# H3 long convolution and SwiGLU on one core: block 0's second norm from PSUM, paired down rows, new instruction orders

## Chip, cores and metric

The kernel runs on one core of one Trainium2 chip. The metric is the device time of one execution in microseconds. Three executions of the kernel before took 274.61 us in the median (273.61 to 275.37).

## What is computed

Two sublayers on a sequence of 2048 tokens with 640 channels, all in bfloat16. `_layernorm` subtracts the mean and divides by the square root of variance plus 1e-5.

```python
def _A_ref(q, k, v, shift_k, ssm_k, ssm_D):
    ...
    for t in range(ks):                                  # ks = 4
        k_shift = k_shift + k_pad[:, t:t + S, :] * shift_k[:, ks - 1 - t][None, None, :]
    kv = k_shift * v
    ...                                                  # y: causal convolution of kv with ssm_k over 2048 tokens, by FFT
    y = y + kv * ssm_D[None, None, :]
    return q * y

def _B_ref(x, w_gate, w_up, w_down):                     # 640 -> 1728 -> 640
    g = _silu(x @ w_gate)
    u = x @ w_up
    return (g * u) @ w_down

x = A_q
h = x + _A_ref(_layernorm(x, axis=-1), A_k, A_v, A_shift_k, A_ssm_k, A_ssm_D)
h2 = h + _B_ref(_layernorm(h, axis=-1), B_w_gate, B_w_up, B_w_down)
```

## The kernel before

The 2048 tokens are cut into four blocks of 512. The long convolution becomes a block convolution: every block of kv (`xf0` to `xf3`) and every block of the filter (`kf0` to `kf3`) is taken through a half-sample-shifted Fourier transform of 512 points by matrix products, spectra are multiplied on VectorE (`prod(j, i)`, for j up to i), and the inverse transform (`iv0` to `iv3`) gives the block's output. The feed-forward layer then runs on the block (`ffn`).

For a block the stages are:

- `kv` (L548, L543, L554): the four-tap filter of k as products with diagonal matrices, on TensorE in 64x64 tiles for the first four channel groups and in one full tile for the fifth, evicted by ScalarE; five transposing DMAs (`kvt`) bring it back to token rows in `kvo`; VectorE multiplies it into `vt` (L563).
- `halves` (L502, L514): eight transforms of four 320-column matmuls, for two frequency halves f, even or odd samples and cosine or sine. ScalarE evicts each; VectorE adds and subtracts even and odd (`bfly`, L491). For `kf0` alone the kernel before is "direct": the odd results aren't evicted, VectorE adds them from PSUM (L510).
- `prod`: products with the filter's spectra (L576, L577), their sums (L579, L581), added to `Y` (L584); behind the last one, `bfly` makes the inputs `IE` and `IO` of the inverse.
- `inverse` (L637): four tiles of 128 tokens. For each, ScalarE copies PSUM with the bias 1/std of the first norm into `qo` (L648), VectorE multiplies with the normalised x (L650) which gives h, ScalarE takes the row sum (L652) and the sum of squared deviations (L654), GpSimd adds epsilon and takes the power -1/2 (L656, L658), VectorE normalises (L660), and a transposing DMA (`hn`) writes `hnT`.
- `ffn`: fourteen groups of hidden rows, thirteen of 128 and one of 64. A group of 128 is ten 512-column matmuls (L681, L682); the last holds 64 gate and 64 up columns in five (L692). ScalarE applies silu (L699) and copies the up part (L701), VectorE multiplies them (L703). The last group's product goes to rows 64 to 127 of `gz`, whose other rows are zero. Then, for four tiles of 128 tokens, 14 row groups times two column halves of 320 are accumulated (L715), VectorE adds the result to h (L721) and SP stores it.

All accumulators come from one pool of four PSUM tiles of two banks each (`units=4`). A tile is taken when the first matmul into it is issued and given back when its last reader is done. ScalarE does most evictions.

Every engine's instruction order is written out. `g.add` gives every operation a number as the program is traced; the `ORDER` lists name these numbers per engine (TensorE, ScalarE, VectorE, GpSimd, and SP for DMA issues), and an engine takes its list strictly in that order, waiting on semaphores. `schedule` only walks through the lists to assign the PSUM tiles. The cost in each `g.add` belongs to the search that made the lists, which isn't part of the program.

In the lists before, TensorE takes all of kv0, kf0 but one transform and four kf1 transforms ahead of xf0; the remaining filter transforms and kv1 stand around iv0; the feed-forward of a block overlaps with the next block's VectorE products.

Of the kernel before, what the change touches and what calls it, by code (L numbers as in the profile page):

```python
# [10 lines left out]
ALU = mybir.AluOpType  # L11
ACTF = mybir.ActivationFunctionType
P = 128
# [15 lines left out]
class _Tile:  # L29
# [8 lines left out]
    def f(self, b, n, parts=slice(0, P)):  # L38
        o = self.unit * 1024 + b * 512
        return self.g.ps[parts, o:o + n]  # L40

# [13 lines left out]
class _Graph:  # L55
# [148 lines left out]
    def emit(self, block):  # L204
# [74 lines left out]
    """,  # L279
    "act": """  # L280
# [10 lines left out]
    """,  # L291
    "dve": """
# [10 lines left out]
    """,  # L303
    "pool": """
        8 5 6 7 147 148 149 150 151 204 205 196 220 197 221 212 213 327 328 329 408 409 400 384 401 392 385 393 506 507 508 581
        597 582 598 589 573 590 574 695 696 697 780 796 781 797 772 773 788 789
    """,
    "sp": """
# [7 lines left out]
def bass_sequential_preLN__ssm_conv_h3__swiglu_ffn__prompt_kernel(  # L316
# [31 lines left out]
    ftab_d = nc.inline_tensor(_to_bf16(np.stack([np.cos(angx), np.sin(angx)], 1).reshape(P, -1)), name="cst_ftab")  # L348
    itab_d = nc.inline_tensor(_to_bf16(np.stack([np.cos(angi), np.sin(angi)], 1).reshape(P, -1)), name="cst_itab")
# [4 lines left out]
    with ExitStack() as es:  # L354
# [56 lines left out]
        KO = [sb("KO%d" % m, p, [2, 2, D]) for m, p in enumerate((w + 10240, S[4], w + 10240, S[4] + 5120))]  # L411
        o = w + 17920
# [4 lines left out]
        mv = [sb("mv%d" % i, o + 320 + 32 * i, [4], f32) for i in range(4)]  # L417
# [3 lines left out]
        BN, DIRECT = (0,), ('kf0',)  # L421
# [26 lines left out]
        load("ftab", ftab[:], ftab_d.ap().rearrange("p (a j c) -> p a j c", a=2, j=4), 524288)  # L448
        load("itab", itab[:], itab_d.ap().rearrange("p (a f j c) -> p a f j c", a=2, f=2, j=4), 524288)
# [5 lines left out]
        g.add("pool", "gz", lambda e: e.memset(gz[0:H, :], 0.0), 500, w=[gz[0:H, :]])  # L455
# [36 lines left out]

        def halves(cls, name, src, ev, od, scale, direct=False):
# [23 lines left out]
        def kfwd(m, dst):  # L517
            halves("kf", "kf%d" % m, KT[m], dst, KO[m], D ** 0.5 / N, "kf%d" % m in DIRECT)
            for f in range(0 if "kf%d" % m in DIRECT else 2):
                bfly("kf%d" % m, dst[:, f], KO[m][:, f], dst[:, f], dst[:, f + 2], 2 * D)  # L520

        def kcomb(dst, own, prev, m):
            g.add("dve", "kc%d" % m, lambda e: e.tensor_tensor(out=dst[:, :, 0, :], in0=own[:, :, 0, :], in1=prev[:, :, 1, :], op=ALU.add),
                  cdve(4 * D), r=[own[:, :, 0, :], prev[:, :, 1, :]], w=[dst[:, :, 0, :]])
            g.add("dve", "kc%d" % m, lambda e: e.tensor_tensor(out=dst[:, :, 1, :], in0=own[:, :, 1, :], in1=prev[:, :, 0, :], op=ALU.subtract),
                  cdve(4 * D), r=[own[:, :, 1, :], prev[:, :, 0, :]], w=[dst[:, :, 1, :]])

        def kv(i):
# [6 lines left out]
            for a in range(3):  # L535
# [17 lines left out]
                ks = kT[:, c0:c0 + nb, 0:N]  # L553
                g.add("act", nm, lambda e, pt=pt, ks=ks, nb=nb: e.activation(  # L554
# [244 lines left out]
```

## Time and profile before

| | |
|---|---|
| median of 3 runs | 274.61 us |
| the profiled execution | 276.58 us |
| its span, first to last instruction | 274.6 us |
| TensorE busy | 255.8 us (93%) |
| VectorE busy | 210.5 us (77%) |
| ScalarE busy | 187.9 us (68%) |
| GpSimd busy | 37.8 us (14%) |
| mean granted TensorE clock | 0.981 |

The profile shows one execution. An instruction's line (L715) is its line in the kernel printed above. Busy time counts when an engine executes; matmuls are pipelined, so that successive ones overlap in the records and the step from start to start is what one costs. An arrow in brackets gives the idle time in front of an instruction and what ended it.

### The profile page before, as it was taken

Reading aid. Unit: us, or ns where it says so; the run is one execution under the profiler, and the core shown is the slowest. Engines: PE = TensorE matmul, PEld = TensorE weight load, DVE = VectorE, ACT = ScalarE, POOL = GpSimd, SP = SyncE. Lnnn points to the kernel's source line nnn. Section 1 sums busy time; section 2 is a strip of 40 time slices with the busy share of each in tenths; the row PEclk is TensorE's granted clock in tenths of the full one; section 3 lists DMA queues with packets and bytes.
Section 4 is the critical chain, followed back from the end, with each engine's and each line's share of the span. In section 5 each row is a group of like instructions: output and inputs, shape, how many; then the busy total and the mean of one; then the engine's idle time right before and its main releaser. Section 6 shows DMA issues by size and latency. Waiting matters only on the chain.

```text
span 274.6 us, 4036 instructions
## 1 busy us (share of the span) xinstructions
PE 255.8 (93%) x1596; PEld 143.4 (52%) x1596; DVE 210.5 (77%) x281; ACT 187.9 (68%) x338; POOL 37.8 (14%) x54
## 2 busy tenths in 40 slices
PE   0998767899899999999999999999999999999995
PEld 0566434354544566754444666644446774444673
DVE  1479997987999999999999999999999413212222
ACT  1798998989966799167978892667769911546400
POOL 1002302900040011100040054000500220000000
PEclk9999989599999999999999999999999999999999
DMA  7999974274900073463100415530000050200002
GB/s 171 318 175 319 381 272 98 48 118 102 376 17 0 0 169 85 94 170 114 46 1 2 98 21 124 143 98 0 0 0 2 1 121 2 72 0 2 0 24 72
DMA packets 45204, 26.49 MB, mean 96 GB/s; under 512 B 34945, under 2 KB 43906, under 8 KB 45186
## 3 DMA queue, kind: packets, MB, share of 16 engines
q1 hardware_dynamic: 44528, 26.23, 35.2%
q8 instruction: 12, 0.20, 0.3%
q10 hardware_dynamic: 658, 0.01, 0.1%
q14 instruction: 6, 0.05, 0.1%
HBM read 15.69 MB, written 2.62 MB: 67 GB/s over the span
## 4 chain that ended last, share of the span: by engine, by line
PE 58%; DVE 25%; ACT 9%; DMA 6%; SPq 1%; issue 1%; DVEq 0%
PE ps L681 16%; PE ps L682 16%; PE ps L715 11%; PE ps L502 6%; DVE tt L577 4%; DMA kvo<-kT 4%; DVE tt L576 4%; PE ps L637 3%; PE ps L548 2%; DVE X L491 2%; DMA ident<-cst_id 2%; DVE xh L721 2%; DVE vt L563 2%; PE ps L692 2%; ACT qo L648 2%; DVE Y L584 2%
## 5 line engine op out<-in xcount | busy, mean ns | idle before, releaser
L715 PE MATMUL ps<-Wd,gu 128*128 128x320 bf16 x416 | 59.6, 299 | 0.0
L681 PE MATMUL ps<-hnT,GA 128*128 128x512 bf16 x140 | 53.1, 379 | 0.2 <-ACT ub L701 0.2
L682 PE MATMUL ps<-hnT,UA 128*128 128x512 bf16 x140 | 53.1, 379 | 0.0
L701 ACT ACTIVATE ub<-ps 128x512 bf16<-128x512 f32 (+1 forms) x56 | 32.8, 596 | 25.5 <-PE ps L682 19.3
L715 PEld LDWEIGHTS ps<-Wd,gu 128*128 128x128 bf16 x416 | 40.5, 98 | 17.0 <-DVE gu L703 0.5
L681 PE MATMUL ps<-hnT,GB 128*128 128x512 bf16 x120 | 45.5, 379 | 0.0
L682 PE MATMUL ps<-hnT,UB 128*128 128x512 bf16 x120 | 45.5, 379 | 0.0
L699 ACT ACTIVATE gu<-ps 128x512 bf16<-128x512 f32 x52 | 30.1, 596 | 13.4 <-PE ps L682 13.2
L703 DVE TENSOR_TENSOR gu<-gu,ub 128x512 bf16<-128x512 bf16 x52 | 21.2, 420 | 23.3 <-ACT gu L699 14.0
L576 DVE TENSOR_TENSOR tt<-X,C 128x2560 bf16<-128x2560 bf16 x20 | 29.7, 1484 | 0.1
L577 DVE TENSOR_TENSOR tt<-X,C 128x2560 bf16<-128x2560 bf16 x20 | 29.7, 1484 | 0.1
L502 PE MATMUL ps<-KT,ftab 128*128 128x320 bf16 x128 | 21.7, 316 | 4.0 <-ACT KT L482 1.6
L721 DVE SCALAR_TENSOR_TENSOR xh<-ps,st,xh 128x640 bf16<-128x640 f32 x16 | 14.0, 879 | 14.4 <-PE ps L715 14.4
L681 PEld LDWEIGHTS ps<-hnT,GA 128*128 128x128 bf16 x140 | 13.7, 98 | 17.3 <-ACT ub L701 0.7
L682 PEld LDWEIGHTS ps<-hnT,UA 128*128 128x128 bf16 x140 | 13.7, 98 | 15.7
L514 ACT ACTIVATE FO<-ps 128x640 bf16<-128x640 f32 x16 | 10.7, 705 | 14.3 <-PE ps L502 14.3
L502 PE MATMUL ps<-vt,ftab 128*128 128x320 bf16 x128 | 18.8, 299 | 1.5 <-DVE vt L563 1.4
L682 PEld LDWEIGHTS ps<-hnT,UB 128*128 128x128 bf16 x120 | 11.8, 98 | 14.2
L681 PEld LDWEIGHTS ps<-hnT,GB 128*128 128x128 bf16 x120 | 11.8, 98 | 14.1
L502 PEld LDWEIGHTS ps<-KT,ftab 128*128 128x128 bf16 x128 | 11.5, 101 | 13.2 <-ACT KT L482 2.7
L656 POOL TENSOR_SCALAR mv<-mv 128x1 f32<-128x1 f32 x16 | 6.6, 418 | 85.5 <-ACT qo L654 85.5
L584 DVE TENSOR_TENSOR Y<-Y,tt 128x2560 bf16<-128x2560 bf16 x12 | 17.8, 1486 | 0.1
(73 smaller groups left out, 377.8 us busy)
## 6 DMA issues: line engine op xcount, KB each, us to landing
kc<-in_A_ssm_k_dram SPq DMA_DIRECT2D x4, 640.0 KB, 5.6
xh<-in_A_q_dram SPq DMA_DIRECT2D x4, 640.0 KB, 5.2
vt<-in_A_v_dram SPq DMA_DIRECT2D x4, 640.0 KB, 6.2
out_dram<-xh SPq DMA_DIRECT2D x16, 160.0 KB, 2.0
Wd<-in_B_w_down_dram SPq DMA_DIRECT2D x1, 1280.0 KB, 6.9
UA<-in_B_w_up_dram SPq DMA_DIRECT2D x1, 1120.0 KB, 10.3
GA<-in_B_w_gate_dram SPq DMA_DIRECT2D x1, 1120.0 KB, 14.6
UB<-in_B_w_up_dram SPq DMA_DIRECT2D x1, 960.0 KB, 10.7
```

The source lines that it names most:

```text
L502: last = e.matmul(pt.f(c, W), ftab[:, cs, j, f * P:(f + 1) * P], src[:, j, c * W:(c + 1) * W], start=(j == par), stop=(j == par + 2))
L514: g.add("act", name, lambda e, pt=pt, d=d: e.activation(out=d.rearrange("p (b x) -> p b x", b=2), in_=pt.f2(W), func=ACTF.Copy, scale=scal ...
L576: g.add("dve", nm, lambda e, x=x, k=k: e.tensor_tensor(out=t1, in0=x, in1=k, op=ALU.mult), cdve(2560), r=[x, k], w=[t1])
L577: g.add("dve", nm, lambda e, x=x, k=ksw: e.tensor_tensor(out=t2, in0=x, in1=k, op=ALU.mult), cdve(2560), r=[x, k], w=[t2])
L584: g.add("dve", nm, lambda e, yy=yy: e.tensor_tensor(out=yy, in0=yy, in1=tacc, op=ALU.add), cdve(2560), r=[yy, tacc], w=[yy])
L681: e.matmul(pt.f(0, N), wg[:, c, f0:f0 + P], hnT[:, c, :], start=(c == 0), stop=(c == NC5 - 1))
L682: last = e.matmul(pt.f(1, N), wu[:, c, f0:f0 + P], hnT[:, c, :], start=(c == 0), stop=(c == NC5 - 1))
L699: g.add("act", nm, lambda e, pt=pt, gv=gv, a=ps_g: e.activation(out=gv, in_=pt.f(a[0], N, a[1]), func=ACTF.Silu, scale=D ** 0.5), cact(N), ...
L701: g.add("act", nm, lambda e, pt=pt, uv=uv, a=ps_u: e.activation(out=uv, in_=pt.f(a[0], N, a[1]), func=ACTF.Copy, scale=D ** 0.5), cact(N), ...
L703: g.add("dve", nm, lambda e, uv=uv, gv=gv: e.tensor_tensor(out=gv, in0=gv, in1=uv, op=ALU.mult), cdve(N), r=[gv, uv], w=[gv])
L715: last = e.matmul(pt.f(c, W), slots[fb][:, j * P:(j + 1) * P], Wd[:, fb, c * W:(c + 1) * W], start=(fb == 0), stop=(fb == 13))
L721: g.add("dve", nm, lambda e, pt=pt, x2=x2, m=m: e.scalar_tensor_tensor(out=x2, in0=pt.f2(W), scalar=m, in1=x2, op0=ALU.subtract, op1=ALU.add),
```

## The change

Operations that are numbered anew, and three edits that change what is executed (the branches for `R4`, `D8`, `PT` and `BN2`, whose switches are empty, add nothing):

- `ST = (0,)`: in block 0's second norm one VectorE `scalar_tensor_tensor` reads the inverse's tile from PSUM, adds the bias, multiplies with x, writes h and its row sum. ScalarE's copy, VectorE's product and ScalarE's row sum go. GpSimd takes the mean from the sum with one more operation a tile; the squares are taken of the row sum minus 640 h, so that epsilon and the scale in front of silu (`gain`) change by powers of 640.
- `PAIR = True`: the last hidden group's product is made in two halves: tokens 0 to 255 in rows 64 to 127 of `gz`, tokens 256 to 511 in rows 0 to 63. The last 64 rows of `Wd` are loaded twice, one half each. In the down product, 13 row groups are accumulated with full tiles; the last 64 rows of token tiles j and j + 2 are done together, one in the upper 64 array rows and one in the lower. The clearing of `gz` goes.
- `DIRECT = ()`: kf0 goes the way of the other transforms: all eight results are evicted by ScalarE and VectorE adds and subtracts in SBUF.
- `ORDER`: all five lists are new.

```diff
-        BN, DIRECT = (0,), ('kf0',)
+        BN, DIRECT, D8, PT, BN2, ST, R4, PAIR = (0,), (), (), (), (), (0,), (), True
...
+                if st:
+                    x2 = x.rearrange("p (b x) -> p b x", b=2)
+                    g.add("dve", nm, lambda e, pt=pt, x2=x2, s=s, j=j, m=m: e.scalar_tensor_tensor(
+                        out=x2, in0=pt.f2(W), scalar=s[:, 3, j:j + 1], in1=x2, op0=ALU.add, op1=ALU.mult, accum_out=m[:, 4:5]),
+                          cps(D) + 120, r=[x, s[:, 3, j:j + 1]], w=[x, m[:, 4:5]], pr=[pt])
+                    g.add("pool", nm, lambda e, m=m: e.tensor_scalar(out=m[:, 0:1], in0=m[:, 4:5], scalar1=-1.0 / D, scalar2=None, op0=ALU.mult),
+                          400, r=[m[:, 4:5]], w=[m[:, 0:1]])
+                    g.add("act", nm, lambda e, x=x, m=m, q=q: e.activation(out=q[:], in_=x, func=ACTF.Square, scale=-float(D), bias=m[:, 4:5],
+                                                                          accum_out=m[:, 1:2]), cact(D, 1) + 115,
+                          r=[x, m[:, 4:5]], w=[q[:], m[:, 1:2]])
...
+                parts = [(rows, ps_g, ps_u, slice(0, N))]
+                if fb == 13 and PAIR:
+                    parts = [(slice(H, P), ps_g, ps_u, slice(0, N // 2)), (slice(0, H), ps_g, ps_u, slice(N // 2, N))]
...
+            for j in ((0, 2, 1, 3) if PAIR else range(4)):
...
+                if PAIR and not second:
+                    dn[j + 2] = g.tile("dn")
+
+                    def mm(e, j=j, ta=dn[j], tb=dn[j + 2]):
+                        for c in range(2):
+                            for t, row, k in ((ta, H, j), (tb, 0, j + 2)):
+                                last = e.matmul(t.f(c, W), gz[row:row + H, k * P:(k + 1) * P], Wd[row:row + H, 13, c * W:(c + 1) * W],
+                                                start=(row == 0), stop=(row == H), tile_position=(row, 0))
+                        return last
...
+        if PAIR:
+            for h in range(2):
+                load("Wd", Wd[H * h:H * h + H, 13, :], B_w_down[F - H:F, :], 81920)
```

The new lists, in the names used above, around the first block:

- TensorE: kv0's third part stands behind six kf0 transforms; one kf1 transform stands ahead of xf0 and four stand inside it; xf0's four f = 0 transforms come first. iv0's first three tiles, three filter transforms, the fourth tile, then ten filter transforms mixed with kv1, and three gu0 groups ahead of xf1 instead of four.
- VectorE: iv0's four PSUM operations with three kf1 additions between the third and the fourth; block 1's product with kv (L563) ahead of the first L703, and five kf additions and product steps behind it.
- SP: one half of the last `Wd` rows ahead of ftab; GB loaded early and GA behind kT1.
- In every block the two pairs stand next to each other, behind the full-tile matmuls of the first two token tiles and ahead of those of the other two.

More of the change, by code (lines that the diff above doesn't have):

```diff
@@ L40, in f, with flat @@
         return self.g.ps[parts, o:o + n]
+    def flat(self, n, at=0):
+        o = self.unit * 1024 + at
+        return self.g.ps[:, o:o + n]
     def f2(self, n):
@@ L491, in bfly, with eighths, mm @@
                 g.add("dve", name, lambda e, d=d, op=op: e.tensor_tensor(out=d, in0=e_, in1=o_, op=op), cdve(n), r=[e_, o_], w=[d])
+        def eighths(cls, name, src, dst, scale):
+            for f in range(4):
+                for cs in range(2):
+                    pt = g.tile(cls)
+                    def mm(e, pt=pt, f=f, cs=cs):
+                        fs = slice((f % 2) * P, (f % 2 + 1) * P)
+                        for j in range(4):
+                            for c in range(2):
+                                tab = ntab[:, cs, j // 2, fs] if f > 1 and j % 2 else ftab[:, cs, j, fs]
+                                last = e.matmul(pt.f(c, W), tab, src[:, j, c * W:(c + 1) * W], start=(j == 0), stop=(j == 3))
+                        return last
+                    g.add("pe", name, mm, cpe(W, 8), r=[ftab[:, cs], src] + ([ntab[:, cs]] if f > 1 else []), pw=[pt])
+                    d = dst[:, f, cs, :]
+                    g.add("act", name, lambda e, pt=pt, d=d: e.activation(out=d.rearrange("p (b x) -> p b x", b=2), in_=pt.f2(W),
+                                                                         func=ACTF.Copy, scale=scale), cact(D), w=[d], pr=[pt])
         def halves(cls, name, src, ev, od, scale, direct=False):
@@ L520, in kfwd, with quarters, mm @@
                 bfly("kf%d" % m, dst[:, f], KO[m][:, f], dst[:, f], dst[:, f + 2], 2 * D)
+        def quarters(cls, name, src, ev, od, scale):
+            for r in range(4):
+                for cs in range(2):
+                    pt = g.tile(cls)
+                    def mm(e, pt=pt, r=r, cs=cs):
+                        for c in range(2):
+                            last = e.matmul(pt.f(c, W), ftab[:, cs, r, 0:P], src[:, r, c * W:(c + 1) * W], start=True, stop=True)
+                        return last
+                    g.add("pe", name, mm, cpe(W, 2), r=[ftab[:, cs], src[:, r, :]], pw=[pt])
+                    d = od[:, r // 2, cs, :] if r % 2 else ev[:, r, cs, :]
+                    g.add("act", name, lambda e, pt=pt, d=d: e.activation(out=d.rearrange("p (b x) -> p b x", b=2), in_=pt.f2(W),
+                                                                         func=ACTF.Copy, scale=scale), cact(D), w=[d], pr=[pt])
@@ new lines, in tt2, with pick, spread @@
+        def tt2(name, op, out, a_, b_):
+            g.add("dve", name, lambda e: e.tensor_tensor(out=out, in0=a_, in1=b_, op=op), cdve(2 * D), r=[a_, b_], w=[out])
+        def pick(t, off, step):
+            return bass.AP(t[:].tensor, t[:].offset + off * D, [list(t[:].ap[0]), [step * D, 2], [1, D]])
+        def spread(name, x, o_):
+            tt2(name, ALU.add, x[:, 1], o_[:, 0], o_[:, 1])
+            tt2(name, ALU.subtract, o_[:, 0], o_[:, 0], o_[:, 1])
+            tt2(name, ALU.add, x[:, 3], x[:, 0], x[:, 2])
+            tt2(name, ALU.subtract, o_[:, 1], x[:, 0], x[:, 2])
+            tt2(name, ALU.add, x[:, 0], x[:, 3], x[:, 1])
+            tt2(name, ALU.subtract, x[:, 2], x[:, 3], x[:, 1])
+            tt2(name, ALU.subtract, pick(x, 2, 5), o_[:, 1], pick(o_, 1, -1))
+            tt2(name, ALU.add, pick(x, 6, -3), o_[:, 1], pick(o_, 1, -1))
@@ L553, in kv, with tr @@
                 ks = kT[:, c0:c0 + nb, 0:N]
+                if i in PT:
+                    g.add("act", nm, lambda e, pt=pt, ks=ks, nb=nb: e.activation(out=ks, in_=pt.f2(N)[:, 0:nb], func=ACTF.Copy),
+                          cact(N * nb), w=[ks], pr=[pt])
+                    tp = g.tile("kt")
+                    def tr(e, tp=tp, c0=c0, nb=nb):
+                        for j in range(4):
+                            for b in range(nb):
+                                src = kT[:, c0 + b, j:j + 509:4]
+                                last = e.matmul(tp.flat(P, P * (nb * j + b)), src, ident[:, 0:P] if b == 0 else iswap, start=True, stop=True)
+                        return last
+                    g.add("pe", nm, tr, 70 * 4 * nb, r=[ks, ident[:, 0:P]], pw=[tp])
+                    d = vt[:, :, P * c0:P * (c0 + nb)]
+                    g.add("dve", nm, lambda e, tp=tp, d=d, nb=nb: e.tensor_tensor(
+                        out=d, in0=tp.flat(4 * P * nb).rearrange("p (j x) -> p j x", j=4), in1=d, op=ALU.mult), cps(4 * P * nb),
+                          r=[d], w=[d], pr=[tp])
+                    continue
                 g.add("act", nm, lambda e, pt=pt, ks=ks, nb=nb: e.activation(
@@ L668, in ffn @@
             nm = "ff%d" % i
+            gain = D ** 1.5 if i in ST else D ** 0.5
             slots = []
@@ L715, in mm @@
                                 last = e.matmul(pt.f(c, W), slots[fb][:, j * P:(j + 1) * P], Wd[:, fb, c * W:(c + 1) * W],
-                                                start=(fb == 0), stop=(fb == 13))
+                                                start=(fb == 0 and not second), stop=(fb == 13 or second and fb == 12))
                         return last
```

133 lines of the change are left out of this document (95 added, 38 removed), and 58 rows, old and new, of the table ORDER.

## The prediction

> **What bounds the kernel now.** I read the busy time by stage first, then the TensorE timeline where that table shows holes. Columns: window, length, busy us (and instructions) of TensorE, its weight loads, VectorE, ScalarE and GpSimd, granted clock, DMA share, GB/s.
>
> ```profile
> 21.40:39.40 18.00, 13.84 (x116) 8.90 (x116) 17.71 (x24) 17.10 (x26) 4.39 (x5) 0.99 1.02 359
> 39.40:60.00 20.60, 17.52 (x109) 9.08 (x110) 18.51 (x24) 17.96 (x36) 8.19 (x8) 0.76 0.39 81
> 60.00:70.00 10.00, 9.30 (x45) 4.20 (x45) 7.77 (x13) 9.97 (x20) 0.00 (x0) 1.00 0.67 140
> 70.00:210.00 140.00, 139.66 (x841) 76.54 (x839) 138.20 (x172) 103.13 (x195) 20.99 (x25) 1.00 0.28 73
> 210.00:271.40 61.40, 61.40 (x371) 35.83 (x368) 17.73 (x35) 26.25 (x51) 3.24 (x8) 1.00 0.11 30
> ```
>
> TensorE has no hole after 70 us: whatever is won must come from its work, or from the first 70 us. But VectorE is as full: 138.2 of 140 us between 70 and 210, so TensorE cannot be pulled forward alone. The timeline shows them meet, TensorE starting right behind VectorE, at the input of block 1's forward transform (L563, then L502) and of the last inverse (L491, then L637):
>
> ```profile
> 68.12 1.28 DVE L563 TENSOR_TENSOR vt<-vt,kvo 128x512 bf16<-128x512 bf16 x2
> ...
> 69.47 4.52 PE L502 MATMUL ps<-vt,ftab 128*128 128x320 bf16 x32 [0.70 <-DVE vt L563]
> 73.82 0.38 PE L681 MATMUL ps<-hnT,GA 128*128 128x512 bf16 x1
> ...
> 208.12 1.55 DVE L491 TENSOR_TENSOR IO<-Y 128x1280 bf16<-128x1280 bf16 x2
> ...
> 209.72 2.52 PE L637 MATMUL ps<-IO,itab 128*128 128x320 bf16 x16
> ```
>
> So the end moves by what VectorE gains up to 209.7, plus what TensorE saves after it. From 69.47 to 73.82 I also take the price of one 320-column matmul: 4.35/32 = 0.136 us, 0.54 for a four-matmul transform.
>
> **The change, part by part.**
>
> *Block 0's transform.* Read off the new lists, the four f = 0 transforms of xf0 come first; before, their results left PSUM second, fourth, fifth and sixth.
>
> ```profile
> 11.48 7.60 SPq L442 DMA_TRANSPOSE kvo<-kT  x5
> ...
> 21.37 2.35 PE L502 MATMUL ps<-vt,ftab 128*128 128x320 bf16 x16 [0.72 <-DVE vt L563]
> 22.13 2.49 ACT L514 ACTIVATE X<-ps 128x640 bf16<-128x640 f32 x4 [0.68 <-PE ps L502]
> 26.17 2.42 DVE L491 TENSOR_TENSOR X<-X,FO 128x1280 bf16<-128x1280 bf16 x3 [0.19 <-ACT FO L514]
> ```
>
> Four evictions end at 22.13 + 2.49 = 24.6, so the VectorE chain of block 0 can start at 24.6 instead of 26.17: **1.5 us**. Its 14.6 us of products are the same. Against this, kv0's third part now stands behind six kf0 transforms on TensorE and five kf0 evictions on ScalarE, and its transpose is the last of the five on SP. Those five take 7.6 us to issue, so the fifth cannot start before about 17; kv0's first two parts are evicted by 13 (before SP's second issue), and five evictions of 0.62 and its own put the third at about 16.8. I take no loss; up to 1 us is possible. Of the two Wd half loads (80 KB each instead of one of 160) one stands ahead of ftab on SP, in front of loads and before the transposes: one more issue, covered by SP's wait for kv0's first eviction.
>
> *kf0 without direct evictions:* eight VectorE operations from PSUM (0.82 us each) become four additions (2.42/3 = 0.81) and four ScalarE evictions (0.62). All of it lies ahead of 24.6, where VectorE has room (9.7 of 15.2 us busy before 21.4); ScalarE pays 2.5 us. No gain taken.
>
> *Second norm of block 0.* Price rows, 39.4 to 60 us, and the two forms of the PSUM operation:
>
> ```profile
> L648 ACT ACTIVATE qo<-ps,st 128x640 bf16<-128x640 f32 x4 | 3.2, 788 | 1.3 <-PE ps L637 1.3
> L652 ACT ACTIVATE qo<-xh 128x640 bf16<-128x640 bf16 x4 | 2.9, 729 | 0.0
> L652 ACT ACTIVATION_READ_ACCUMULATOR qo<-xh 128x1 f32 x4 | 0.8, 191 | 0.0
> L650 DVE TENSOR_TENSOR xh<-xh,qo 128x640 bf16<-128x640 bf16 x4 | 2.0, 498 | 1.6 <-ACT qo L648 1.6
> L577 DVE TENSOR_TENSOR tt<-X,C 128x2560 bf16<-128x2560 bf16 x2 | 3.0, 1481 | 0.0
> L656 POOL TENSOR_SCALAR mv<-mv 128x1 f32<-128x1 f32 x4 | 2.8, 699 | 16.8 <-ACT qo L654 16.8
> L510 DVE SCALAR_TENSOR_TENSOR C<-ps,C 128x640 bf16<-128x640 f32 x8 | 6.5, 817 | 0.7 <-ACT C L514 0.7
> L721 DVE SCALAR_TENSOR_TENSOR xh<-ps,st,xh 128x640 bf16<-128x640 f32 x16 | 14.0, 879 | 14.4 <-PE ps L715 14.4
> ```
>
> ScalarE loses L648 and L652: 6.9 us, less the 2.5 above. VectorE gives up four L650 (2.0 us) for four operations whose sum output no row shows: at least L510's 0.82, at most L721's 0.88 plus an accumulator read of 0.19 as ScalarE's, 1.07. So 1.3 to 2.3 us more; I take **2.2**, since L721 has the same pointer scalar and the sum must be read out. In return VectorE no longer waits for ScalarE here. Its longest waits between 40.8 and 69.4 us, and that stretch as a whole:
>
> ```profile
> 42.58 0.49 DVE L650 TENSOR_TENSOR xh<-xh,qo 128x640 bf16<-128x640 bf16 x1 [1.03 <-ACT qo L648]
> ...
> 55.26 0.45 DVE L660 TENSOR_SCALAR qo<-xh,mv 128x640 bf16<-128x640 bf16 x1 [0.46 <-POOL mv L658]
> ...
> 65.24 0.43 DVE L703 TENSOR_TENSOR gu<-gu,ub 128x512 bf16<-128x512 bf16 x1 [1.61 <-ACT ub L701]
> ```
>
> ```profile
> 40.80:69.40 28.60, 24.89 (x144) 12.05 (x142) 24.28 (x34) 25.93 (x51) 8.19 (x8) 0.85 0.49 98
> ```
>
> The stretch holds 28.6 - 24.3 = 4.3 us of idle. The waits for L648 go with it; the longest goes because the new list puts block 1's kvmul (L563) ahead of the first gmul (L703); I leave 1.0 for new ones: **3.3** back. GpSimd gets four more small operations for the mean (0.7 us each at this stage's L656 mean); they run beside ScalarE's squares, and the normalisations (L660) that need them have products and k additions between them.
>
> Sum at kvmul1: 1.5 + 3.3 - 2.2 = **2.6 us**. Can TensorE follow? iv0 starts at 37.9; four iv, thirteen k transforms and kv1 are 14.5 us, to 52.4. On VectorE the first PSUM operation starts at 40.1 (iv0's first tile 1.1 us, one addition), four of them and three additions end at 46.5, four normalisations (0.4) with three operations of L577's size between end at 52.5; the transpose lands 2.6 later (hnT row): gu0 at 55 instead of 59.96. Three gu0 groups of ten 0.216 matmuls end at 61.5; kvmul1, since the new list puts 4.7 us of additions and products behind it, at 69.4 - 2.6 - 4.7 = 62.1. TensorE waits about 0.6 us: VectorE decides. GA's load is moved behind kT1's transposes, at about 44; the DMA engines are 39% busy there, so its 1120 KB land before 55, if the issue row's 14.6 us, taken at full queues, does not repeat (44 + 14.6 = 58.6: still before 59.96).
>
> *Pairs.* The two transfers just named, then TensorE around kv2, where 64x64 tiles are used, and its last down group:
>
> ```profile
> hnT<-qo SPq DMA_TRANSPOSE x16, 2.6
> GA<-in_B_w_gate_dram SPq DMA_DIRECT2D x1, 1120.0 KB, 14.6
> ...
> 101.39 0.98 PE L715 MATMUL ps<-Wd,gu 128*128 128x320 bf16 x6
> 102.21 0.43 PE L715 MATMUL ps<-Wd,gz 128*128 128x320 bf16 x2
> 102.57 1.92 PE L548 MATMUL ps<-kT,dg 64*64 64x512 bf16 x32
> 104.43 1.04 PE L543 MATMUL ps<-kT,dl 128*128 128x512 bf16 x4
> 105.30 0.30 PE L715 MATMUL ps<-Wd,gu 128*128 128x320 bf16 x1
> ...
> 267.44 3.69 PE L715 MATMUL ps<-Wd,gu 128*128 128x320 bf16 x26
> 270.97 0.43 PE L715 MATMUL ps<-Wd,gz 128*128 128x320 bf16 x2
> ```
>
> A full 512-column matmul takes (105.30 - 104.43)/4 = 0.217 us. The 32 small ones of that length start within 1.86 us; one by one they would take 6.9, so four run at once, and I take two 64x128 ones to run at once. The step into the mode costs 102.57 - 102.21 - 2 x 0.136 = 0.09, the step out about as much: eight steps of 0.217 make 1.74 of the 1.86. A round trip is about 0.21. A block loses eight 0.136 matmuls (1.09) and gains four slots (0.54) and, since the new list has both pairs next to each other, one round trip: **0.33 us less**. If halves do not overlap: 0.21 more. The pairs hold four PSUM tiles at once, all there are; the seven matmul groups ahead of them are time enough for kv's evictions. The split of the last gmul into two halves costs VectorE 0 to 0.3 a block, I take 0.08.
>
> [...]
>
> *Sum.* 2.6 at kvmul1; 0.8 of the 1.8 us that VectorE idles from 70 to 210; less 0.24 for three split gmuls: 3.2 at 209.7. Behind it blocks 2 and 3 save 0.33 each: **3.9 us**. The profiled execution took 276.58 us with a span of 274.6 (2.0 around it), so 272.7 on its own scale; it lay 2.0 above the median of the runs shown, 274.61, and on that scale the forecast is **270.7**, 269.2 (the 2.2 at 1.3, and 0.6 more of the waits back) to 271.9 (0.2 more lost, and the input 1.0 late).
>
> **The rivals.**
>
> *A cold TensorE at the start.* The granted clock falls to half behind thin stretches:
>
> ```profile
> 17.00:20.70 3.70, 3.29 (x23) 1.68 (x20) 2.75 (x6) 3.49 (x6) 0.00 (x0) 1.00 0.71 76
> 36.00:39.40 3.40, 1.31 (x8) 0.62 (x8) 3.40 (x6) 3.40 (x7) 0.00 (x0) 0.94 0.93 354
> 39.40:43.00 3.60, 3.60 (x16) 2.17 (x17) 2.57 (x5) 2.52 (x5) 0.00 (x0) 0.58 0.03 10
> 46.00:49.40 3.40, 1.04 (x4) 0.31 (x4) 3.37 (x3) 3.40 (x11) 2.98 (x3) 0.98 0.48 109
> 49.40:55.40 6.00, 5.36 (x32) 2.10 (x36) 5.50 (x9) 5.99 (x11) 5.21 (x6) 0.50 0.34 64
> ```
>
> 39% and 31% busy were thin enough. The new list takes three kf1 transforms (1.6 us) from the stretch before xf0: 1.66 busy from 17 to 21.4, 38%. At half clock the four transforms take 2.2 more and eat the 1.5: 272.2. [...]
>
> *TensorE decides, not VectorE:* if VectorE's waits after 60 us vanish too, the 5.0 us at gu0 and four blocks of 0.33 count: 268.3. Against: VectorE's 138 of 140.
>
> *Pairs that do not run side by side:* blocks 2 and 3 cost 0.42 instead of saving 0.66: 271.8. Against: the 32 matmuls above.
>
> *Slower: TensorE, ahead of VectorE, idles in lumps.* Its list is fixed, so where it waits for VectorE at xf1, xf2, xf3 and iv3 for over about 1.6 us in a stretch, the clock halves for 3.4 us and costs 1.7, as at 39.4. The first lump eats slack; with all four, 6.8 us go, against the 3.9 of the forecast: 277.5. For: two such lumps stand in the trace now. Against: gu groups of 2.2 us fill the lists around these points.
>
> **How the numbers follow.** Forecast 0.45, cold start 0.22, TensorE decides 0.10, pairs 0.07, lumps 0.16. A measurement of this kernel tells about 1% from no change. Below 271.9 lie nearly all of the first, third and fourth and a third of the cold start: 0.61; above 277.4 more than half of the lumps: 0.11; within 1%: 0.28. The range 267.8 to 275.2 leaves out the lumps and the lowest tail.
>
> **What would show it.** Right: the first block 0 addition (L491, X) near 24.6; the four PSUM operations at 0.9 to 1.1 us; gu0's first matmul near 55; iv3 near 206.5; pair matmuls two at a time, 0.136 a step; 6.9 us less of L648 and L652. Wrong: xf0 at a clock under 1.0, a VectorE idle over 2 us between 40 and 62, holes in TensorE after 70, or gu0 not before 58.

## The result, and the profile after

The changed kernel took **292.46 us** (median of four runs, 292.31 to 295.01) against 274.99 (273.61 to 275.74) for the kernel before on the same chip: a ratio of **1.067, 95% interval 1.060 to 1.073**. It is slower, where 270.7 was forecast. (Ratios here leave disturbed executions out on both sides, so they are not always the quotient of the two medians.) The profiled execution took 295.01 us with a span of 293.0.

The busy time by stage first, in the columns of the prediction's first table (length, TensorE, weight loads, VectorE, ScalarE, GpSimd, granted clock, DMA share, GB/s):

```profile
27.70:60.00 32.30, 26.82 (x219) 16.06 (x218) 30.50 (x40) 29.42 (x46) 10.03 (x14) 1.00 0.76 213
60.00:82.20 22.20, 20.95 (x110) 10.29 (x109) 21.12 (x29) 19.26 (x38) 0.00 (x0) 1.00 0.46 144
82.20:95.00 12.80, 9.38 (x44) 4.05 (x42) 12.70 (x14) 4.26 (x8) 12.78 (x1) 1.00 0.00 0
95.00:103.00 8.00, 4.39 (x17) 2.52 (x18) 0.85 (x2) 4.24 (x7) 1.87 (x2) 0.57 0.00 0
103.00:209.70 106.70, 104.33 (x653) 56.90 (x652) 101.90 (x130) 75.48 (x151) 19.49 (x20) 1.00 0.31 69
209.70:220.60 10.90, 10.82 (x57) 5.28 (x55) 10.79 (x13) 4.29 (x9) 10.89 (x1) 1.00 0.00 0
220.60:232.50 11.90, 6.32 (x28) 3.59 (x29) 3.83 (x8) 8.72 (x15) 1.87 (x2) 0.71 0.01 2
```

Before, TensorE had no hole after 70 us. Now there are two, at 90 to 103 and 220 to 232, and the clock halves in both (0.57 and 0.71 as the mean of the stretches, 0.50 for 6.8 us in each). What is striking is the GpSimd column: in the stretch ahead of each hole it is busy from end to end with one single instruction. The groups of the page name it, and ScalarE's wait for it:

```profile
L719 POOL TENSOR_SCALAR st<-st 128x4 f32<-128x4 f32 x4 | 26.6, 6647 | 84.3 <-ACT jk L716 84.2
L728 ACT ACTIVATE xh<-xh,st 128x640 bf16<-128x640 bf16 x16 | 14.6, 933 | 14.3 <-POOL st L724 14.3
```

L719 adds epsilon to 128x4 numbers, the row sums of squares of a block's first norm. The same instruction before (timeline of GpSimd and VectorE, kernel before; L613 is that line there):

```profile
77.60 1.49 DVE L576 TENSOR_TENSOR tt<-X,C 128x2560 bf16<-128x2560 bf16 x1
79.00 0.82 DVE L581 TENSOR_TENSOR tt<-tt 128x1280 bf16<-128x1280 bf16 x1
...
78.54 0.64 POOL L613 TENSOR_SCALAR st<-st 128x4 f32<-128x4 f32 x1 [23.31 <-ACT jk L610]
```

And in block 1 of the changed kernel, timelines of GpSimd, VectorE, ScalarE and TensorE one after the other:

```profile
82.21 12.78 POOL L719 TENSOR_SCALAR st<-st 128x4 f32<-128x4 f32 x1 [26.70 <-ACT jk L716]
95.07 1.67 POOL L722 TENSOR_TENSOR st<-st,half 128x8 f32<-128x8 f32 x1
...
82.12 1.48 DVE L680 TENSOR_TENSOR tt<-X,C 128x2560 bf16<-128x2560 bf16 x1
83.52 0.81 DVE L500 TENSOR_TENSOR IO<-Y 128x1280 bf16<-128x1280 bf16 x1
...
93.42 1.48 DVE L602 TENSOR_TENSOR C<-C,R 128x2560 bf16<-128x2560 bf16 x1
98.50 0.42 DVE L840 TENSOR_TENSOR gu<-gu,ub 128x512 bf16<-128x512 bf16 x1 [3.60 <-ACT ub L838]
...
97.06 0.92 ACT L728 ACTIVATE xh<-xh,st 128x640 bf16<-128x640 bf16 x1 [7.72 <-POOL st L724]
97.89 0.58 ACT L838 ACTIVATE ub<-ps 128x512 bf16<-128x512 f32 x1
...
98.61 4.36 PE L745 MATMUL ps<-IO,itab 128*128 128x320 bf16 x16 [7.03 <-ACT ub L838]
```

Before, GpSimd's add ended 0.09 us after the VectorE operation during which it was asked for. Now it ends 0.10 us after the thirteenth operation behind that one (94.99 against 94.90): it got in only when VectorE had nothing left to do. ScalarE's list has the normalisation L728 ahead of the copies L838, so ScalarE stands still for 7.72 us, no PSUM tile is freed, TensorE waits 7.03 us, and the sixteen matmuls behind it run at half clock (4.36 us for 2.2). VectorE went dry because its next product (L840) waits for ScalarE's copy L838. So GpSimd waits for VectorE, ScalarE for GpSimd and VectorE for ScalarE, and the circle opened only when VectorE had run out of other work. Block 3 repeats it (10.89 us from 209.70).

### The profile page after: what moved, and what is told of

It is laid out like the page before. It is cut to its first block, busy times and chain, and to the rows that moved or that the text cites. A ratio compares the mean times of both kernels' runs of the same rounds, so it can differ in the third digit from the quotient of the medians.

```text
span 293.0 us, 4053 instructions
## 1 busy us (share of the span) xinstructions
PE 258.5 (88%) x1596; PEld 142.3 (49%) x1596; DVE 209.0 (71%) x285; ACT 184.3 (63%) x338; POOL 62.8 (21%) x57
## 4 chain that ended last, share of the span: by engine, by line
PE 47%; ACT 17%; DVE 13%; POOL 12%; DMA 8%; issue 1%; SPq 1%
PE ps L813 12%; PE ps L814 11%; PE ps L857 10%; POOL st L719 8%; PE ps L529 6%; PE ps L745 4%; ACT ub L838 3%; DMA kvo<-kT 2%; ACT xh L728 2%; POOL mv L789 2%; DMA hnT<-qo 2%; DMA xh<-in_A_q_dram 2%; DMA ident<-cst_id 2%; ACT gu L836 1%; ACT qo L768 1%; ACT qo L781 1%
## 5 line engine op out<-in xcount | busy, mean ns | idle before, releaser
L857 PE MATMUL ps<-Wd,gu 128*128 128x320 bf16 x416 | 58.4, 299 | 0.0
L838 ACT ACTIVATE ub<-ps 128x512 bf16<-128x512 f32 (+1 forms) x60 | 33.5, 567 | 25.6 <-PE ps L814 20.8
L719 POOL TENSOR_SCALAR st<-st 128x4 f32<-128x4 f32 x4 | 26.6, 6647 | 84.3 <-ACT jk L716 84.2
L840 DVE TENSOR_TENSOR gu<-gu,ub 128x512 bf16<-128x512 bf16 x52 | 21.0, 419 | 31.7 <-ACT ub L838 19.7
L529 PE MATMUL ps<-vt,ftab 128*128 128x320 bf16 x128 | 21.8, 326 | 3.3 <-DVE vt L660 3.3
L745 PE MATMUL ps<-IO,itab 128*128 128x320 bf16 x64 | 12.6, 362 | 13.6 <-ACT ub L838 12.6
L728 ACT ACTIVATE xh<-xh,st 128x640 bf16<-128x640 bf16 x16 | 14.6, 933 | 14.3 <-POOL st L724 14.3
L529 PE MATMUL ps<-KT,ftab 128*128 128x320 bf16 x128 | 20.4, 301 | 2.3 <-ACT KT L491 1.2
L785 POOL TENSOR_SCALAR mv<-mv 128x1 f32<-128x1 f32 x16 | 11.4, 710 | 49.3 <-ACT qo L783 49.0
```

The lines of the kernel that those rows point to most:

```text
L529: last = e.matmul(pt.f(c, W), ftab[:, cs, j, f * P:(f + 1) * P], src[:, j, c * W:(c + 1) * W], start=(j == par), stop=(j == par + 2))
L719: g.add("pool", nm, lambda e: e.tensor_scalar(out=s[:, 2, :], in0=s[:, 1, :], scalar1=LN_EPS * D, scalar2=None, op0=ALU.add), 3000 if i el ...
L728: g.add("act", nm, lambda e, j=j, xj=xj: e.activation(out=xj, in_=xj, func=ACTF.Identity, scale=s[:, 4, j:j + 1], bias=s[:, 5, j:j + 1]), ...
L745: last = e.matmul(pt.f(c, W), itab[:, cs, f, j, :], src[:, j // 2 if len(fs) == 1 else f, cs, c * W:(c + 1) * W], start=(f == 0 and cs == ...
L838: g.add("act", nm, lambda e, pt=pt, uv=uv, a=ps_u, ts=ts: e.activation(out=uv, in_=pt.f(a[0], N, a[1])[:, ts], func=ACTF.Copy, scale=gain) ...
L840: g.add("dve", nm, lambda e, uv=uv, gv=gv: e.tensor_tensor(out=gv, in0=gv, in1=uv, op=ALU.mult), cdve(n), r=[gv, uv], w=[gv])
```

## The experiments

The theory (A in the expectations): GpSimd is shut out by VectorE's unbroken stream of operations with two SBUF inputs, and what hangs on it is late. The rivals: the new lists starve TensorE by themselves, through PSUM and ScalarE's order, and GpSimd's long record is a symptom (B); or the edits themselves cost the time (C).

**1. GpSimd not needed in blocks 1 to 3.**

```
- g.add("pool", ... (s1 + eps); pow; mul ...)        # i > 0
+ g.add("dve", ... s3 = (s1 + eps) * c; s4 = (s1 + eps) * c2; s5 = s0 * s4 ...)
```

The power is left out here; a multiplication stands in its place.

> The changed kernel, but the three small GpSimd operations behind the row sums of blocks 1 to 3 (add epsilon, power, multiply) run on VectorE, two or three places into the stream where the row sums become ready; the power is replaced by a multiplication, so the values are not the norm's. Theory A (GpSimd is shut out by VectorE's unbroken stream of two-input operations, and ScalarE's evictions stand behind the normalisation that waits for GpSimd): both TensorE stalls, near 90 and 217 us, and the half-clock stretches behind them go, some 17 us: 272 to 277 us. Theory B (the new lists starve TensorE by themselves, through PSUM and ScalarE's order, and GpSimd's long record is only a symptom): 288 to 293.

**276.38 us**, 1.006 of before (1.003 to 1.009). The two stretches that held the holes, by stage:

```profile
95.00:103.00 8.00, 7.72 (x72) 4.36 (x72) 7.94 (x12) 7.95 (x17) 2.22 (x1) 1.00 0.25 57
220.60:232.50 11.90, 11.54 (x72) 6.76 (x71) 3.30 (x6) 2.13 (x6) 1.24 (x3) 1.00 0.39 98
```

TensorE is busy 7.72 of 8.00 us (4.39 before this edit) and 11.54 of 11.90 (6.32), at full clock. Theory A holds, B does not.

**2. Nothing taken away, nine tiny operations added.**

```
+ g.add("dve", tensor_scalar(out=bst[:, 0:4], in0=bst[:, 4:8], scalar1=1.0, op0=mult))   # 3 in each of blocks 1-3
```

> The changed kernel with three tiny one-input VectorE operations (128x4) put into VectorE's list in each of blocks 1 to 3, behind the point where GpSimd's add of epsilon becomes ready; nothing is taken away, nine operations are added. Theory A: GpSimd gets in at the first or second of them, its add ends within 3 us instead of 12.8 and 10.9, and the time falls to 273 to 278. Theory B: no less than 290. A third possibility, that only a real idle time of VectorE lets GpSimd in: add still over 8 us and time as the changed kernel.

**276.44 us**, ratio 1.001 (0.997 to 1.006): adding work to the engine that is full saves 16 us. GpSimd's and VectorE's timelines in block 1 (L691 is the added operation, L683 the add of epsilon):

```profile
81.59 1.51 POOL L683 TENSOR_SCALAR st<-st 128x4 f32<-128x4 f32 x1 [26.71 <-ACT jk L680]
83.19 2.48 POOL L686 TENSOR_TENSOR st<-st,half 128x8 f32<-128x8 f32 x1
...
81.50 1.48 DVE L644 TENSOR_TENSOR tt<-X,C 128x2560 bf16<-128x2560 bf16 x1
82.91 0.16 DVE L691 TENSOR_SCALAR bst<-bst 128x4 f32<-128x4 f32 x1
82.98 0.82 DVE L464 TENSOR_TENSOR IO<-Y 128x1280 bf16<-128x1280 bf16 x1
```

The request came during the same product as in the changed kernel, and there the next operation, L500's butterfly, kept GpSimd out. Here the first one-input operation lets it in at 82.91 + 0.19.

**3 and 4. The new lists without two of the edits, and the edits with the old lists.** In the third the lists are the new ones, with the tasks of block 0's norm and of the last down rows as before; in the fourth the lists are the old ones with the new tasks in the places of those that they replace.

> The new lists without two of the source edits: block 0's second norm as before (ScalarE evicts and sums), last down rows one group after the other with zero rows as before; block 0's kernel transform through ScalarE as in the changed kernel. Theory A: VectorE's stream and ScalarE's order in blocks 1 and 3 are the changed kernel's, so the stalls stay: 288 to 296, GpSimd's add over 6 us in at least one block. Theory C (the pair matmuls or the PSUM operations cost the time): 273 to 278.

> Both named edits (second norm of block 0 from PSUM with the row sum, down rows in pairs) with the lists of before, changed only where the tasks differ; block 0's kernel transform as before. Theory A: GpSimd gets in as before and nothing stalls; TensorE saves about 0.3 us a block, VectorE pays 2 us in block 0 and loses its waits for ScalarE there: 271 to 276. Theory C: over 280.

Third: **302.07 us**, 1.100 (1.094 to 1.106), GpSimd's adds 12.78, 2.42 and 10.89 us: the same stall without the PSUM norm and the pairs. That is more than the 288 to 296 expected: in its profile TensorE has one hole more, 4.32 us ahead of 174.61 in block 2, where it waits for the last group's product, which stands undivided at the place of its second half. Fourth: **279.61 us**, 1.021 (1.015 to 1.027), its adds 0.64, 1.00 and 1.59 us (0.64, 0.59 and 1.59 before). So the new order makes the two stalls, and neither of the two edits is needed for them. (The third edit, kf0's way out of PSUM, went with the lists in both.) But my 271 to 276 for the fourth was wrong; experiments 6 and 7 take it apart.

**5. The start, and two more breaks.**

```
  sp order:  kT0  Wd13a  ftab ...  Wd13b      ->   kT0  ftab ...  Wd13a  Wd13b
  dve order: p02.0im  p02.0t1                 ->   p02.0im  brk  p02.0t1   (the like in block 2)
```

> The changed kernel with the nine tiny one-input VectorE operations of the second experiment, one more in blocks 1 and 2 each where GpSimd's epsilon for the first group's second norm was held 3.6 and 2.2 us (VectorE then waited 0.77 us), and the first half of the last down rows loaded late, beside the second half, instead of ahead of the transform table. Theory A, with the start as the remaining loss: block 0's first addition near 24.5 to 25.5 instead of 27.1, two waits of 0.77 gone, so 2 to 3 us less than the second experiment: 272.5 to 275. If the start and these waits are hidden by TensorE: 275.5 to 277.

**275.52 us**, 1.003 (0.999 to 1.007); 272.5 to 275 was expected. Block 0's first addition came at 25.6 instead of 27.1. Of the two breaks, block 1's worked (its epsilon 0.66 us instead of 3.54), block 2's let nothing in (2.25 us, as without it). The time cannot be told from the second experiment's, nor from the kernel before: no version of the new order that I tried beats the old one.

**6 and 7. The old lists with one edit each.**

> The lists of before with the pairs alone (block 0's norm as before). If the pairs save 0.33 us a block behind the last inverse as forecast, 273.5 to 275; if the old lists, with the pairs' four PSUM tiles held at once, make TensorE wait for evictions, 276 to 279, with a hole in TensorE in a down stretch behind iv3.

> The lists of before with block 0's second norm from PSUM alone (pairs as before). VectorE pays 1.5 us more there and waits less for ScalarE (1.6 us), but in the old places the normalisations wait for GpSimd's longer chain: 275 to 278, slower than before by what VectorE idles between 46 and 62 us. If the old lists leave room: 273 to 275.

Pairs alone **276.95 us**, 1.006 (1.001 to 1.011); PSUM norm alone **278.25 us**, 1.012 (1.004 to 1.020). Neither pays in the old places. With the pairs, TensorE waits behind block 2's down groups for block 3's transposed input (TensorE's timeline of the sixth, then of the fourth experiment):

```profile
226.00 0.39 PE L777 MATMUL ps<-hnT,GA 128*128 128x512 bf16 x1 [1.60 <-DMA hnT<-qo]
```

```profile
229.88 0.38 PE L778 MATMUL ps<-hnT,UA 128*128 128x512 bf16 x1 [1.56 <-DMA hnT<-qo]
```

Counted from TensorE's first matmul on IE (209.89 in the sixth, 212.08 before), the work up to the hole takes 14.51 us instead of 14.80: the pairs save their 0.3. But the transposed input comes at 16.11 us, where it was there at 14.80 before. Most of that delay stands in VectorE's list, sixth experiment, then the kernel before:

```profile
217.00 0.88 DVE L838 SCALAR_TENSOR_TENSOR xh<-ps,st,xh 128x640 bf16<-128x640 f32 x1 [1.01 <-PE ps L833]
217.80 0.80 DVE L755 TENSOR_SCALAR qo<-xh,mv 128x640 bf16<-128x640 bf16 x2
```

```profile
218.13 0.88 DVE L721 SCALAR_TENSOR_TENSOR xh<-ps,st,xh 128x640 bf16<-128x640 f32 x1
218.92 0.80 DVE L660 TENSOR_SCALAR qo<-xh,mv 128x640 bf16<-128x640 bf16 x2
```

The first down sum stands ahead of the normalisation. With the pairs its result is ready only behind two token tiles' full matmuls, so VectorE waits 1.01 us there, and the normalisation and the transpose with it. The old order fits the old down product. With the PSUM norm, block 0's first addition came at 25.6, but block 1's input transform started at 71.6 instead of 69.5; the cause of that was not tried further.

**8. One break, late.** The changed kernel with a single added operation in block 1, nine operations behind the request.

> The changed kernel with a single tiny one-input VectorE operation, in block 1, nine operations behind the point where GpSimd becomes ready. Theory A: GpSimd's add of epsilon there lasts until that operation, 7.5 to 8 us instead of 12.8; block 3's keeps its 10.9; ScalarE's wait falls by about 5 us: 284 to 288. If GpSimd is held for another reason than VectorE's stream, the add keeps 12.8 us and the time 291 to 294.

**293.23 us** (two runs): my time was wrong, the mechanism was not. GpSimd's and VectorE's timelines:

```profile
80.04 7.87 POOL L683 TENSOR_SCALAR st<-st 128x4 f32<-128x4 f32 x1 [26.69 <-ACT jk L680]
87.99 6.34 POOL L686 TENSOR_TENSOR st<-st,half 128x8 f32<-128x8 f32 x1
...
87.69 0.17 DVE L691 TENSOR_SCALAR bst<-bst 128x4 f32<-128x4 f32 x1
...
91.31 1.48 DVE L566 TENSOR_TENSOR C<-C,R 128x2560 bf16<-128x2560 bf16 x1
```

The add ends at 87.91, just behind the break at 87.69. But the next instruction, the power L686, is shut out in its turn until VectorE runs dry at 92.79. Here the add and the power each needed a way in of its own (held 7.87 and 6.34 us); I had counted one.

**9. ScalarE's list.** In blocks 1 and 3 the normalisations L728, and the evictions of the inverse that need GpSimd too, stand behind the last copies and silus.

> The changed kernel, with ScalarE's first-norm normalisations of blocks 1 and 3, and the two evictions of the inverse that need GpSimd too, moved behind the last silu and copy evictions of the gate and up groups, and VectorE's operations that wait for them moved behind the last gate products; nothing is added or removed. If the stall is made of both (GpSimd shut out, and ScalarE's list standing behind it), GpSimd stays shut out, even longer, until VectorE runs out of other work (its add 12 us or more), but TensorE goes on meanwhile: most of the 16 us come back, 276 to 284. If ScalarE's place does not matter, 290 to 294.

**291.3 us**, 1.057 (1.051 to 1.064), the second of the two outcomes. GpSimd's timeline:

```profile
82.22 13.45 POOL L683 TENSOR_SCALAR st<-st 128x4 f32<-128x4 f32 x1 [26.71 <-ACT jk L680]
...
207.48 13.57 POOL L683 TENSOR_SCALAR st<-st 128x4 f32<-128x4 f32 x1 [30.89 <-ACT jk L680]
```

It was shut out even longer, and the holes moved to the inverse's evictions, which wait for it too (4.57 us ahead of 226.40 in block 3). Moving ScalarE's normalisation did not bring the time back; letting GpSimd in did (experiments 1 and 2).

**10. A warm start.**

```
  pe order:  kf1.f0es  kf0.f0es  xf0...   ->   kf1.f0es  kf1.f0oc  kf1.f1es  kf0.f0es  xf0...
```

> The fifth experiment (changed kernel with ten short one-input operations and the late load), with two kernel transforms of block 1 put ahead of block 0's input transform on TensorE and their evictions ahead on ScalarE. If the half clock at block 0's transform costs the start 1 to 1.5 us and VectorE carries that to the last inverse: 273 to 275, with the transform at full clock. If not: as the fifth, 275 to 276.

**276.73 us**, 1.007 (1.003 to 1.011): nothing won. In the profiled execution (280.32 us) the transform did run at full clock, 24 matmuls in 3.42 us, and block 0's first addition came at 24.71, so the edit did what it was meant to. Why the time did not follow stays open.

**11 to 13. The shut-out by itself.** Why was the add let in at the first handover before, and at none of thirteen after? The three programs do none of the reference's work: VectorE runs streams, GpSimd is asked for the same small operation at set moments.

> None of the reference's work: 40 trials of about 6 us. In each VectorE runs eight operations back to back while GpSimd is asked for one 128x4 operation at a moment set by a ScalarE copy of 256 to 1152 elements. Kinds: A, two-input bf16 128x1280, no waits between them; B, the same, each waiting for the one before; C, two-input 128x2560 and 128x512 in turn; D, as A but the fifth operation has one input; E, as A with GpSimd's power of two inputs. If a missed first handover means waiting for a pause: GpSimd's record in A, B, C and E is either under 1.5 us or runs to the end of the eight (4 to 6 us), in D at most to the fifth operation (2 to 3 us). If each handover is a fresh chance: a spread of ends over all handovers.

> None of the reference's work: 24 trials of ten VectorE operations back to back, at the kernel's addresses, with GpSimd's add of epsilon of block 1 (128x4, at its address) asked for while they run, at six moments each. G: the sequence of the changed kernel where the add was held 12.8 us (products, butterflies and gate products of block 1); H: the sequence of the kernel before where it got in at the first handover; A: ten plain 128x1280 operations; C: 128x2560 and 128x512 in turn. If the operands of the sequence decide: held to the end of the ten (6 to 9 us) in G at all moments, under 1.6 us in H. If the moment of the request decides: some of six held in G and in H. If the other engines' traffic decides, none is held in any kind (all under 1.6 us), as in the first measurement.

> None of the reference's work: the changed kernel's VectorE sequence of the last measurement, 35 trials; GpSimd's add is now asked for by a ScalarE square with a row sum, as in the kernel. Kind 0: nothing else runs; 1: ScalarE goes on copying from PSUM without a pause; 2: TensorE runs 36 matmuls of 512 columns; 3: both; 4: GpSimd is asked only in every third trial, so that it has been idle some 27 us, as in the kernel. If ScalarE's or TensorE's traffic makes GpSimd miss the handovers: records to the end of the ten (6 to 8 us) in 1, 2 or 3 and under 1.6 us in 0 and 4. If GpSimd's long idle time does: 6 to 8 us in 4 alone. If neither: under 1.6 us in all 25, and why the kernel's handovers are missed stays open.

The groups of the three pages, GpSimd's rows:

```profile
L77 POOL TENSOR_SCALAR st<-st 128x4 f32<-128x4 f32 x32 | 19.6, 611 | 34.1 <-ACT j L85 34.1
L75 POOL TENSOR_TENSOR st<-st,half 128x4 f32<-128x4 f32 x8 | 11.0, 1371 | 7.2 <-ACT j L85 7.2
```

```profile
L186 POOL TENSOR_SCALAR st<-st 128x4 f32<-128x4 f32 x24 | 15.9, 663 | 234.4 <-ACT GA L196 234.4
```

```profile
L190 POOL TENSOR_SCALAR st<-st 128x4 f32<-128x4 f32 x25 | 14.3, 574 | 325.9 <-ACT jk L213 325.9
```

In the first, GpSimd ran ahead of the trials that were meant to pace it, so that all 40 requests came during the streams of kinds A and B; kinds C and D were not tested, and the power of kind E (L75) fell into B's. In all three, no add was held longer than 1.46 us. Each ended some 0.08 us behind the end of the VectorE operation it met, or of the next one where it was asked for too late (0.11 us ahead was too late, but for one add, and 0.16 was not). So the blocking for one operation is shown 81 times. The shut-out over many operations did not show: not with the same sequence at the same addresses, not with ScalarE's or TensorE's traffic, not with the row sum as the trigger, not with GpSimd idle for 22 us ahead of it. **What decides whether GpSimd gets in at the first handover stays open.** In the kernels' traces two things are regular. An add that was asked for in time and still missed its first handover got in when VectorE idled, or its operations overlapped by 40 ns or less instead of some 80; at an added one-input operation (but for block 2's added one in the fifth and tenth); or, once, ahead of an operation from PSUM. And it is a matter of the program, not of chance: changed kernel and third experiment, 12.78 and 10.89 us both. But the neighbours do not decide. Block 2's first add of the second norm, asked for 0.42 us ahead of the same handover between the same two operations, got in at once before and in the seventh experiment, and was held 4.4 us longer in the fourth and the sixth, the two with the pairs. So an edit too can bring a shut-out, in the old order.

## Why the prediction was wrong, by its own steps

**The step that failed** is what the forecast took GpSimd to cost: it priced GpSimd's instructions by their durations before, as if these were constants, and only in block 0 (four more small operations that "run beside ScalarE's squares"). ScalarE's wait for GpSimd in blocks 1 and 3 was put at nothing: L613 (0.64, 0.59 and 1.59 us before) was no term of the sum, because nothing in the diff touches it but a planner's cost. Yet the new order puts other VectorE operations beside it, and the same instruction took 12.78, 2.69 and 10.89 us. Experiments 1 and 2 put a price on it: 292.46 - 276.4 = **16 us**. That the step failed is shown; why GpSimd was kept out over so many operations is not.

**Lumps.** The rival on the slower side had the right form, TensorE idle in lumps with half clock behind them, among them at iv3; not its place at iv1, nor its cause, and 277.5 was far too little, because I sized the lump by VectorE's waits of before. Its figures come from one hole of before (TensorE's timeline, then the stretch at half clock):

```profile
39.41 3.81 PE L637 MATMUL ps<-IO,itab 128*128 128x320 bf16 x16 [1.61 <-DVE IO L491]
```

```profile
39.00:42.41 3.41, 3.00 (x12) 1.74 (x13) 2.56 (x4) 2.78 (x6) 0.00 (x0) 0.50 0.07 26
```

The 1.6 us is the length of that hole; no run shows it as a limit. In blocks 1 and 3 of the changed kernel the clock was at 0.50 for 6.8 us each, not 3.4.

**The start.** 24.6 was forecast for block 0's first addition; it came at 27.35. TensorE's timeline, changed kernel, then the third experiment, where the last down rows load late in one piece:

```profile
22.13 5.52 PE L529 MATMUL ps<-vt,ftab 128*128 128x320 bf16 x20 [2.90 <-DVE vt L660]
```

```profile
21.08 2.89 PE L493 MATMUL ps<-vt,ftab 128*128 128x320 bf16 x20 [1.47 <-DVE vt L624]
```

With the half load ahead of ftab on SP the input came 1.05 us later ("I take no loss; up to 1 us is possible"). In the other kernels that load it there it came at 21.42 to 23.18, in the fifth experiment, which loads it late, at 20.89; so about 1 us fits. Behind the thin stretch (TensorE busy 0.56 of 3.46 us from 18.67 to 22.13) the granted clock was 0.50 to 27.70: 5.52 us for twenty matmuls, against 2.89. This is the cold-start rival, as priced, and it does not hang on the load alone: the eighth experiment, with the load ahead, took 2.89 too, and the fifth, without it, 4.39. Where neither happened the addition came at 24.36: the 1.5 us of the step were there to be had.

**The PSUM operations.** Timeline of VectorE, changed kernel:

```profile
43.21 0.87 DVE L759 SCALAR_TENSOR_TENSOR xh<-ps,st,xh 128x640 bf16<-128x640 f32 x1
44.01 0.08 DVE L759 DVE_READ_ACCUMULATOR xh<-ps,st,xh 128x1 f32 x1
44.01 0.87 DVE L759 SCALAR_TENSOR_TENSOR xh<-ps,st,xh 128x640 bf16<-128x640 f32 x1
...
50.93 0.45 DVE L791 TENSOR_SCALAR qo<-xh,mv 128x640 bf16<-128x640 bf16 x1 [0.47 <-POOL mv L789]
```

From start to start 0.80 us, the sum's read-out (0.08) hidden: four cost 4 x (0.80 - 0.42) = 1.5 us more (0.42: L650's 0.50 less the 0.08 by which neighbours overlap), not 2.2; the lower half of the bounds was right.

**VectorE's waits.** Without the stall, in the second experiment, VectorE's chain from block 0's first addition to the input of iv3, split at the start of block 1's transform; first the kernel before:

```profile
26.17:69.47 43.30, 35.35 (x231) 18.43 (x229) 38.95 (x49) 40.63 (x71) 11.91 (x11) 0.88 0.64 181
69.47:211.81 142.34, 142.00 (x856) 78.03 (x857) 140.54 (x175) 105.42 (x199) 20.99 (x25) 1.00 0.28 73
```

```profile
27.14:66.30 39.16, 32.08 (x242) 18.33 (x242) 37.19 (x49) 34.89 (x56) 11.13 (x14) 1.00 0.76 210
66.30:212.70 146.40, 143.05 (x854) 77.06 (x863) 143.54 (x190) 107.18 (x212) 28.26 (x25) 1.00 0.27 65
```

VectorE idled 4.35 and 1.80 us before, 1.97 and 2.86 now: 2.4 won in the first part (I had 3.3), 1.1 lost in the second (I had 0.8 won). GpSimd is in this too: the normalisation of the second norm (L791) waits 0.46 us for its power L789 three times in the first part. The 4.1 us by which the first part is shorter are given back in the second, which got work from it: the whole chain is 185.56 us long, against 185.64. It keeps that length in the fifth experiment, 184.95 us, where it starts 1.58 us earlier. That fits the forecast's "VectorE decides", though the busy times of the second part do not show it by themselves (143.5 us for VectorE, 143.1 for TensorE, of 146.4). But of the 2.6 at kvmul1 nothing reaches iv3: 212.70 where 206.5 plus two additions were forecast.

**The pairs** were right. Timeline of TensorE, changed kernel:

```profile
117.55 0.72 PE L869 MATMUL ps<-Wd,gz 64*128 64x320 bf16 x8
118.20 7.24 PE L857 MATMUL ps<-Wd,gu 128*128 128x320 bf16 x52
```

Eight in 0.65 us from start to start: four slots of 0.136 and 0.11 for the way out of the mode. Behind iv3, from VectorE's last sum to the end, 274.64 - 211.81 = 62.83 us before, 274.89 - 212.70 = 62.19 in the second experiment: 0.64 saved, 0.66 forecast; the order behind iv3 is new as well, so not all of it need be the pairs'. The old order cannot use them (experiment 6).

**gu0** came at 58.6, not 55. VectorE's last normalisation ended at 56.0 instead of 52.5: the start came 2.75 late and the three waits for L789 took 1.4, of which the cheaper PSUM operations gave some back. The transpose behind it took the 2.6 of the forecast.

**One operation, or fourteen.** In the last three programs no add was held longer than 1.46 us. Held no longer than that, L719 would by my estimate have left the changed kernel near the second experiment's 276.44 us, where the adds took 1.51, 1.19 and 0.63 us; it was held for 12.78 us, over fourteen operations.

## What to carry to other kernels

The same small GpSimd instruction took 0.64 us in one order and 12.78 us in another beside a full VectorE: in a reordered kernel look, for each of its results, at what VectorE runs behind the request, and at whose list stands behind the result. Where the result matters, put a short operation with one input (128x4 here) behind the request in VectorE's list, one for each GpSimd instruction of the chain, and read in the trace whether it let it in; here nine at 0.07 us each bought 16, and one alone left the power shut out for 6.34 us. And an order searched with fixed costs does not know this, so a new order is a change to every engine's waits, even where the diff touches none of its operations.

## What the runs showed of the hardware that I had not expected

- GpSimd was shut out over fourteen consecutive two-input VectorE operations (12.78 us; 13.57 over still more in the ninth experiment) though VectorE's records show a handover every 0.3 to 1.4 us; a 128x4 one-input operation mostly ended it (with three of them a block the adds took 1.51, 1.19 and 0.63 us in the second experiment; block 2's added one in the fifth let nothing in, 2.25 us). What decides between this and the first handover is not found.
- VectorE's sum beside an operation from PSUM was nearly free here: a record of 0.87 us and a read-out of 0.08 that the next one hides, and L721, the same form without a sum, had 0.88.
- The granted clock stays at half for 6.8 us in one piece, though TensorE is busy for 4.16 and 5.04 us of it: from 95.94 in block 1, inside the hole of 7.03 us, and from 225.65 in block 3, between those of 3.63 and 1.98.

```profile
95.94:102.77 6.83, 4.16 (x16) 2.42 (x17) 0.85 (x2) 4.24 (x7) 1.01 (x2) 0.50 0.00 0
225.65:232.47 6.82, 5.04 (x20) 2.85 (x21) 2.26 (x5) 5.69 (x12) 0.00 (x0) 0.50 0.00 1
```
